# Low parts by VectorE, masks first, and other ranks for merged parts, in a fused attention and mixing kernel

## The chip, the core and the metric

The kernel runs on one core of one Trainium2 chip. The metric is the device time of one execution in microseconds (us); the figure quoted is the median of several runs. The engines are named as in the profile: PE is TensorE (PEld its weight loads), DVE is VectorE, ACT is ScalarE, POOL is GpSimd, SP is SyncE, which here only issues transfers.

## The reference

Three blocks follow each other, on batch 4, sequence 576, model width 512, all in fp32:

```python
# 1. attention in a window of 64, 8 heads of 64
scores = q @ k.T / 8;  keep 0 <= i - j < 64;  x = softmax(scores) @ v
# 2. four causal attention experts on x (width 64 each), the best two of four by a gate
q, k, v = x @ wq[e], x @ wk[e], x @ wv[e]
out += gate[e] * (softmax(causal(q @ k.T / 8)) @ v) @ wo[e]
# 3. mixing over tokens and channels
theta = x @ w_theta;  zr, zi = x * cos(theta), x * sin(theta)
u = x + w_tok_r @ zr + w_tok_i @ zi
return u + relu(u @ w_ch)
```

## The kernel before

**High and low parts.** Where fp32 accuracy is wanted, an operand is held as two tiles: a rounded high part, and a low part that is the difference. `split` (L101) makes them: one engine, mostly ScalarE, copies the high part (L103), another subtracts it from the source (L106). `mm3` (L108) then makes three matmuls of a product: high by high, high by low, low by high (L109 to L111). So each product needs both parts of both operands, and the low part is made after the high part.

**Stages.** Per batch b and, in the later stages, per half dh of the model width:
- `phase_a(b, hps)`: the windowed attention of block 1, in units of three blocks; scores to a bank (L297), mask and row minimum on VectorE (L305, which reads the masks ma0 and ma1 in the tile cst), exponential on ScalarE (L313), normalising on GpSimd (L320), transposes (L325, with the identity, also in cst), their copy pv (L328 on VectorE or L330 on ScalarE).
- `qk`, `vg_gates`, `attn(b, ep)`, `wo(b)`: projections, gates, the causal attention of two experts, and the output product of block 2. In `attn`, L493 scales by row on GpSimd or VectorE; the transposed diagonal block is copied on VectorE (L512) or ScalarE (L514).
- `fuse`: the product of wo and w_theta, in parts (tile wot). `load_tok`, `load_theta`, `load_ch`: weights, changed from float64 to parts.
- `theta(b, dh)`: angles (bank th), rounding on ScalarE and VectorE (L671, L672), sine and cosine on ScalarE (L674 to L676), product with the transposed x (bank xk) on VectorE (L679, or L693 for the last 64 tokens). For the first three halves the result is split into z (L683). For the other five, `sums_of` (L617) forms the operands of a Strassen product from two token tiles: X, W, Y and V, each with a high part on ScalarE; the low parts of X, W, Y are made at L627, L632 and L636, that of V at L644, and four sums and differences run on VectorE in between (L628, L629, L633, L637). It is called twice per half.
- `mix(b, dh)` for the first three halves and `mix7(b, dh)` for the other five: the product over tokens. Its banks are added to x2T by VectorE (L717, L785), and the sum u is split into cu (L718, L787). `halves` and `halves_end` make the differences of the token weights that `mix7` needs.
- `channel(b)`: the product over channels (bank c), read by VectorE (L843), then out.

**Order.** `merge` (L50) interleaves the parts of a stage: each part is a generator with a total; it yields costs, and the part whose (lead + cost so far) / total is smallest goes next. A larger total means that a part is taken earlier; a negative entry of LEAD puts a part in front, a positive one puts it back, as a share of its total. Parts are numbered in the order in which they are handed over, 0 to 67. This order gives ranks alone: at build time a planner simulates the engines and puts, on each engine, the ready instruction with the best rank next. On the chip each engine, and each engine's transfer queue, then runs its list in that fixed order. A PSUM bank is taken again only when its last reader is done (as 1, ta 1, g 2, bs 2, tb 2 banks).

**The start.** L251 to L254 issue the first transfers: on ScalarE's queue the first 256 columns of k (L251), then identity and masks together (L252); on SP's queue q and the rest of k. The next q and k tiles follow on SP's queue.

Of the kernel before, what the change touches and what calls it, by code (L numbers as in the profile page):

```python
# [23 lines left out]
DM = H * D  # L24
E = 4
NP = H // 2
KN = {'AT': [12.77, 1.06, 85.51, 5.4, 87.1, 55.86, 41.05, 4.07], 'QK': [15.5, 22.07, 12.32, 8.99, 4.97, 0.81, 9.98, 20.79, 20.6], 'VG': [18.37, 4.28, 3.79, 19.87], 'WO': [15.86, 4.2, 6.97, 88.79], 'PA': [11.6, 8.71, 12.47, 1.24, 2.53, 3.58, 5.67], 'TW': [0.76, 0.04, 2.9, 0.42, 2.07], 'CW': [14.78, 12.49, 0.86, 2.63, 1.4, 0.04, 1.33], 'SC': [5, 4, 5, 3, 0, 2, 1, 1], 'BD': [2, 1, 2, 1], 'PV': [0, 1, 2, 1], 'VB': [4, 0, 0, 2], 'WB': [0, 0, 0, 1], 'SB': 3, 'TB': 3, 'WOI': 0, 'AS': [0, 2, 1, 2], 'WE': [[0, 0], [0, 3], [0, 1]], 'XE': [0, 1, 1, 1], 'QB': [0, 1, 0, 0, 0, 0, 0, 0], 'DM': [1, 0, 0], 'DH': [1, 0, 0], 'DL': [0, 0, 1], 'BC': [1, 0, 1, 1], 'LT': 2, 'DP': [1, 1, 1], 'KC': 0, 'WM': 448, 'TC': [8.48, 13.11, 6.04, 7.5, 25.58, 9.0]}
TP = [8.14, 8.0]
CT = ("tb", "bs")
WARM = 2  # L30
LEAD = {19: 0.001, 22: -0.122, 29: 0.129, 35: -0.015, 36: -0.102, 38: 0.359, 42: 0.118, 43: 0.028, 51: -0.277, 54: 0.015, 67: -0.07}
MG = [20, 14.0, 4, 5, 12, 12, 13.0, 13.0, 13.0, 13.0, 13, 12]
TK0 = 1
THS = [[], [0], [], [1], [2], [3], [], []]
NB = S // 64
# [30 lines left out]
def kernel(ctx, tc, qT, kT, vw, consts, w_in, w_o, w_th, w_tk, w_ch, outT):  # L66
# [176 lines left out]
    def fetch(b, hp):  # L243
        if b == 0 and hp % 2:
            qt = bp.tile([P, D, NB], F32, tag="oh", bufs=3, name=f"qt{b}{hp}")
        else:
            qt = ap.tile([P, D, NB], F32, tag="qt", name=f"qt{b}{hp}")
        kt = ap.tile([P, S + 64], F32, tag="kt", bufs=2, name=f"kt{b}{hp}")
        if b == 0 and hp == 0:

            nc.scalar.dma_start(kt[:, :256], kT[b, hp, :, :256])  # L251
            nc.scalar.dma_start(cst[:, : 3 * P], consts[:, : 3 * P])  # L252
            nc.sync.dma_start(qt, qT[b, hp])
            last_load[0] = nc.sync.dma_start(kt[:, 256:], kT[b, hp, :, 256:])  # L254
        elif b == 0:
            nc.sync.dma_start(qt, qT[b, hp])
            last_load[0] = nc.sync.dma_start(kt, kT[b, hp])
        else:
            with tc.issue_after(last_v[0].ins):
                last_load[0] = nc.sync.dma_start(kt, kT[b, hp])  # L260
                nc.sync.dma_start(qt, qT[b, hp])
        return qt, kt
# [354 lines left out]
    def sums_of(b, dh, i, ang):  # L617
        A11, A21, A12, A22 = (ang[:, :, q, k] for q in range(2) for k in range(2))
        if i == 1:
            Z[b, dh] = {}  # L620
        ops = Z[b, dh]
        n = f"{b}{dh}{i}"
        st = (rp if i == 1 else kp).tile([P, 2, 2, P], F32, tag="z", name=f"s{n}")
        s1, s2 = st[:, :, 0], st[:, :, 1]
        x = operand(f"X{n}")
        nc.scalar.copy(out=x[1][:, 0], in_=ang[:, :, :, 0])
        p = nc.gpsimd.tensor_sub(out=x[1][:, 1], in0=ang[:, :, :, 0], in1=f32(x[1][:, 0]))  # L627
        nc.vector.tensor_add(out=s1, in0=A21, in1=A22)  # L628
        nc.vector.tensor_sub(out=s2, in0=s1, in1=A11)  # L629
        w = operand(f"W{n}")  # L630
        nc.scalar.copy(out=w[1][:, 0], in_=st)
        nc.gpsimd.tensor_sub(out=w[1][:, 1], in0=st, in1=f32(w[1][:, 0]))  # L632
        nc.vector.tensor_sub(out=A21, in0=A11, in1=A21)  # L633
        y = operand(f"Y{n}")
        nc.scalar.copy(out=y[1][:, 0], in_=ang[:, :, :, 1])
        nc.gpsimd.tensor_sub(out=y[1][:, 1], in0=ang[:, :, :, 1], in1=f32(y[1][:, 0]))  # L636
        nc.vector.tensor_sub(out=A12, in0=A12, in1=s2)  # L637
        if i == 1:
            tag = free.pop(0)
            ops["V"] = tag, slot(tag, [P, 2, 4, P], f"V{n}")  # L640
        v = ops["V"][1]
        sl = slice(i - 1, i + 1)
        nc.scalar.copy(out=v[:, 0, sl], in_=A12)
        nc.vector.tensor_sub(out=v[:, 1, sl], in0=A12, in1=f32(v[:, 0, sl]))  # L644
        for k, t in zip("XWY", (x, w, y)):
            ops[k, i // 2] = t
        return p

    def theta(b, dh):
        x2 = x2T[b]  # L650
        dsl = slice(dh * HW, dh * HW + HW)
        for i in range(4 if b % 2 else 5):
            n = f"{b}{dh}{i}"
            if i < 4:
                tok = slice(i * P, i * P + P)
                o = ring[8 * b + 4 * dh + i]
                load_o(1)
                x32, ow = (lambda c: x2[:, c, tok]), [o[:, k] for k in range(4)]
            else:
                xt, xo = XT[0]  # L660
                x32, ow = (lambda c: xt[:, c]), [xo[:, k] for k in range(4)]
            th = bank([P, HW], "bs", f"th{n}")
            for c in range(2):
                mm3(th, ow[2 * c], ow[2 * c + 1], GT[c][0][:, dsl], GT[c][1][:, dsl], c == 0, c == 1)
            xk = bank([P, HW], "tb", f"xk{n}")
            for c in range(2):
                nc.tensor.transpose(xk[:, c * P : (c + 1) * P], x32(2 * dh + c), ident)
            if i % 2 == 0:
                ang = bp.tile([P, 2, 2, HW], F32, tag="bms", bufs=2, name=f"ang{n}")
            rn, sn = ang[:, i % 2, 0], ang[:, i % 2, 1]  # L670
            nc.scalar.activation(out=rn, in_=th, func=AF.Identity, bias=magic)  # L671
            nc.vector.scalar_tensor_tensor(out=rn, in0=rn, scalar=-MAGIC, in1=th,  # L672
                                           op0=ALU.add, op1=ALU.subtract)
            nc.scalar.activation(out=sn, in_=rn, func=AF.Sin, scale=-TWO_PI)  # L674
            nc.scalar.activation(out=rn, in_=rn, func=AF.Abs)
            nc.scalar.activation(out=rn, in_=rn, func=AF.Sin, bias=halfpi, scale=-TWO_PI)  # L676
            if i < 4:
                both = ang[:, i % 2]
                d = nc.vector.tensor_mul(out=both, in0=xk.unsqueeze(1).to_broadcast([P, 2, HW]), in1=both)  # L679
                if 2 * b + dh < 3:  # L680
                    zt = slot(first[8 * b + 4 * dh + i], [P, 2, 2, HW], f"z{n}")
                    Z[b, dh, i] = zt
                    mark[b, dh, i] = d, split(zt[:, :, 0], zt[:, :, 1], both, nc.scalar, nc.gpsimd)  # L683
                elif i % 2:
                    mark[b, dh, i] = d, sums_of(b, dh, i, ang.rearrange("p j q (k n) -> p j q k n", k=2))
            else:
                for k in range(2):
                    zt = kp.tile([P, 1, 2, HW], F32R, tag=f"zt{k}{dh}", name=f"z{n}{k}")
                    Z[b + k, dh, i] = zt
                    z = (rp, kp)[k].tile([P, HW], F32, tag="z", name=f"zf{n}{k}")  # L690
                    r = slice(64 * k, 64 * k + 64)
                    for q, tr in enumerate((rn, sn)):
                        nc.vector.tensor_mul(out=z[64 * q : 64 * q + 64], in0=xk[r], in1=tr[r])  # L693
                    split(zt[:, 0, 0], zt[:, 0, 1], z, nc.scalar, nc.gpsimd)
            yield 1.5

    def mix(b, dh):
        x2 = x2T[b]
        if dh == 0:
            UH[b] = hl_set(utags, f"cu{b}")  # L700
        uh, ul = UH[b]
        y = [bank([P, 288], tag, f"y{b}{dh}{k}") for k, tag in enumerate(("g", "g", "as", "ta"))]
        for c in range(9):
            zt = Z[b, dh, c // 2]
            q = c % 2 if c < 8 else 0
            for k in range(4):
                n, mm = divmod(k, 2)
                sl = slice(288 * n, 288 * n + 288)
                ms = slice(mm * P, mm * P + P)
                mm3(y[k], zt[:, q, 0, ms], zt[:, q, 1, ms], wkh[c][:, sl], wkl[c][:, sl],  # L710
                    c == 0, c == 8)
            yield 1.45
        for k in range(4):
            n, mm = divmod(k, 2)
            m = 2 * dh + mm
            sl = slice(288 * n, 288 * n + 288)
            nc.vector.tensor_add(out=x2[:, m, sl], in0=y[k], in1=x2[:, m, sl])  # L717
            split(uh[m][:, sl], ul[m][:, sl], x2[:, m, sl], nc.scalar, nc.gpsimd)  # L718

    def halves():  # L720
        f1 = rp.tile([P, 4, 288], F32, tag="x2b", name="t1")
# [35 lines left out]
    def mix7(b, dh):  # L757
# [26 lines left out]
        def add(m, sl, g, ready=False):  # L784
            nc.vector.tensor_add(out=x2[:, m, sl], in0=g, in1=x2[:, m, sl])  # L785
            if ready:
                split(uh[m][:, sl], ul[m][:, sl], x2[:, m, sl], nc.scalar, nc.gpsimd)  # L787

        def spread(u, *homes):
            for m, sl in homes:  # L790
# [246 lines left out]
```

## Time and profile before

| | |
|---|---|
| median of 3 runs | 502.05 us (500.07 to 503.29) |
| the profiled execution | 501.43 us |
| its span, first to last instruction | 499.6 us |
| PE, PEld busy | 475.9, 446.2 us |
| DVE, ACT, POOL busy | 381.6, 342.2, 319.3 us |
| granted TensorE clock | 1.00 in every stretch |

The span is what the profile shows; the execution's time holds 1.8 us more around it. In the trace, phase_a for batch 0 fills the first 40 us or so, the stages of block 2 follow until about 285 us, and theta, mix, mix7 and channel take the rest. In a row of busy time, the number in brackets after it counts instructions. Matmuls overlap in the records, so a single matmul's time is longer than the step from one to the next.

### The profile page before, as it was taken

To read this page: it belongs to the slowest core of one execution; us is meant where nothing else is said; L and a number is where in the kernel's file an instruction comes from. 1 tells how busy PE (TensorE), PEld (TensorE's weight loads), DVE (VectorE), ACT (ScalarE), POOL (GpSimd) and SP (SyncE) were. 2 spreads that over 40 slices of the span, in tenths; PEclk is the share of its full clock that TensorE was granted. 3 is DMA by queue.
4 is the path that set the end of the run, shared out by engine and by line. 5 is a ranking of instruction groups with operands and counts; after the bars stand their busy time and mean duration, and the time that the engine had idled before them with its cause. 6 is when DMAs were issued, how large, how long until landed. Compare 5 with 4: busy or idle time off the path is not lost.

```text
span 499.6 us, 12071 instructions
## 1 busy us (share of the span) xinstructions
PE 475.9 (95%) x4128; PEld 446.2 (89%) x4128; DVE 381.6 (76%) x1283; ACT 342.2 (68%) x1054; POOL 319.3 (64%) x411
## 2 busy tenths in 40 slices
PE   7899899999999997999989999899999989999997
PEld 5689788999999897998878799899999989999997
DVE  6868989867779659877898969977668948893843
ACT  7948688867878756868787897876167717752620
POOL 6758789674776770323694556679558925891770
PEclk9999999999999999999999999999999999999999
DMA  8564253431316234112235953231362044202002
GB/s 272 182 227 134 67 179 108 139 100 49 125 60 198 78 97 147 33 38 92 88 120 168 349 176 144 71 78 43 100 175 65 23 143 131 65 22 96 2 0 96
DMA packets 45614, 55.92 MB, mean 112 GB/s; under 512 B 6641, under 2 KB 34289, under 8 KB 45553
## 3 DMA queue, kind: packets, MB, share of 16 engines
q1 hardware_dynamic: 44688, 52.46, 33.6%
q10 hardware_dynamic: 864, 2.69, 1.4%
q8 instruction: 33, 0.54, 0.4%
q14 instruction: 29, 0.23, 0.2%
HBM read 43.34 MB, written 11.80 MB: 110 GB/s over the span
## 4 chain that ended last, share of the span: by engine, by line
PE 52%; DVE 18%; ACT 15%; POOL 6%; issue 5%; DMA 3%; SPq 0%; DVEq 0%; ACTq 0%; POOLq 0%
PE as L297 3%; PE bpt L504 3%; ACT ams L313 2%; PE c L109 2%; PE c L110 2%; PE c L111 2%; PE apt L325 2%; PE qk L109 2%; PE bs L472 2%; PE qk L110 2%; PE ao L168 2%; PE qk L111 2%; PE bs L474 2%; PE o L522 2%; DMA wst<-in_dram 1%
## 5 line engine op out<-in xcount | busy, mean ns | idle before, releaser
L320 POOL TENSOR_TENSOR ams<-ams,arc 128x384 f32<-128x384 f32 x48 | 40.4, 845 | 34.4 <-DVE arc L319 14.3
L313 ACT ACTIVATE ams<-ams,anm 128x128 f32<-128x128 f32 x144 | 56.5, 396 | 4.0 <-DVE anm L305 2.9
L481 ACT ACTIVATE bms<-bms,bnm 64x64 f32<-64x64 f32 (+4 forms) x80 | 44.9, 562 | 13.1 <-DVE bnm L476 13.1
L297 PE MATMUL as<-kt,QD 128*128 128x128 f32 x288 | 41.2, 281 | 2.7 <-DVE anm L305 2.5
L297 PEld LDWEIGHTS as<-kt,QD 128*128 128x128 f32 x288 | 36.0, 192 | 6.2 <-DVE anm L305 2.9
L96 POOL TENSOR_SCALAR QD<-qt 64x576 f32<-64x576 f32 x24 | 30.6, 1274 | 11.7 <-DMA qt<-in_dram 4.6
L305 DVE CUSTOM_DVE_ANT_0 ams<-as,cst 128x128 f32<-128x128 f32 x144 | 34.1, 283 | 4.9 <-PE as L297 2.7
L476 DVE CUSTOM_DVE_ANT_0 bms<-bs,mb 64x64 f32<-64x64 f32 (+4 forms) x80 | 32.5, 422 | 5.4 <-PE bs L474 3.7
L106 POOL TENSOR_TENSOR cu<-x2T,cu 128x288 fp32r<-128x288 f32 x32 | 28.3, 901 | 9.9 <-ACT cu L103 9.8
L493 POOL TENSOR_SCALAR bpd<-bms,bsm,gw 128x64 f32<-128x64 f32 (+1 forms) x46 | 20.4, 445 | 20.2 <-DVE bsm L486 8.7
L109 PE MATMUL y<-wkh,z 128*128 128x288 f32 x108 | 32.1, 303 | 0.8 <-DVE x2T L717 0.8
L472 PE MATMUL bs<-KA,QS 128*128 128x288 f32 (+4 forms) x96 | 31.0, 331 | 1.1 <-DVE bnm L476 1.0
L110 PE MATMUL y<-wkl,z 128*128 128x288 f32 x108 | 31.9, 297 | 0.0
L679 DVE TENSOR_TENSOR ang<-xk,ang 128x512 f32<-128x512 f32 x32 | 21.6, 686 | 13.0 <-ACT ang L676 10.8
L111 PE MATMUL y<-wkh,z 128*128 128x288 f32 x108 | 30.9, 297 | 0.0
L671 ACT ACTIVATE ang<-th,magic 128x256 f32<-128x256 f32 x36 | 16.7, 470 | 18.8 <-PE th L111 17.7
L791 POOL TENSOR_TENSOR x2T<-x2T,u 128x288 f32<-128x288 f32 x20 | 16.9, 855 | 19.7 <-DVE u L802 18.1
L504 PE MATMUL bpt<-cst,bms 128*128 128x128 f32 x160 | 27.5, 276 | 1.5 <-ACT oh L103 1.5
L493 POOL TENSOR_SCALAR bms<-bms,bsm,gw 128x384 f32<-128x384 f32 (+3 forms) x38 | 24.7, 650 | 5.9 <-ACT wtuk L138 3.8
L474 PE MATMUL bs<-KL,QS 128*128 128x288 f32 (+4 forms) x96 | 28.4, 302 | 0.0
L313 ACT ACTIVATION_READ_ACCUMULATOR ams<-ams,anm 128x1 f32 x144 | 27.6, 192 | 0.0
L843 DVE SCALAR_TENSOR_TENSOR x2T<-c,x2T 128x288 f32<-128x288 f32 x32 | 13.8, 453 | 16.9 <-PE c L111 16.8
(337 smaller groups left out, 2051.7 us busy)
## 6 DMA issues: line engine op xcount, KB each, us to landing
vt<-in_dram SPq DMA_DIRECT2D x48, 192.0 KB, 2.9
or<-od SPq DMA_DIRECT2D x32, 256.0 KB, 3.3
kt<-in_dram SPq DMA_DIRECT2D x15, 320.0 KB, 3.1
qt<-in_dram SPq DMA_DIRECT2D x16, 288.0 KB, 3.6
out_dram<-x2T SPq DMA_DIRECT2D x32, 144.0 KB, 1.8
w64k<-in_dram SPq DMA_DIRECT2D x5, 576.0 KB, 4.2
od<-oh SPq DMA_DIRECT2D x8, 288.0 KB, 2.7
od<-ol SPq DMA_DIRECT2D x8, 288.0 KB, 2.8
```

Of the source, the lines that this page charges most:

```text
L109: nc.tensor.matmul(out, wh, xh, start=first, stop=False)
L110: nc.tensor.matmul(out, wh, xl, start=False, stop=False)
L111: nc.tensor.matmul(out, wl, xh, start=False, stop=last)
L297: nc.tensor.matmul(s[:, i, :], qd[:, blk], kt[:, 64 * blk : 64 * blk + 128], start=True, stop=True)
L305: nc.vector.tensor_tensor_reduce(out=ms[:, i, :], in0=s[:, i, :], in1=ma0 if (g == 0 and i == 0) else ma1, scale=-0.125, scalar=3.0e38, op ...
L313: nc.scalar.activation(out=ms[:, i, :], in_=ms[:, i, :], func=AF.Exp, bias=nm[:, i : i + 1], scale=-1.0, accum_out=sm[:, i, 0:1],)
L320: nc.gpsimd.tensor_mul(out=ms, in0=ms, in1=rc.unsqueeze(2).to_broadcast([P, 3, P]))
L472: nc.tensor.matmul(s[:, : z - a], qs[:, q0 : q0 + P], ka[:, a:z], start=True, stop=False)
L474: nc.tensor.matmul(s[:, : z - a], qs[:, q0 : q0 + P], KL[e][:, a:z], start=False, stop=True)
L481: ex = nc.scalar.activation(out=ms[:m, :w], in_=ms[:m, :w], func=AF.Exp, bias=nm[:m, ci : ci + 1], scale=-1.0, accum_out=ss[:m, i, 0:1])
L493: eng.tensor_scalar(out=dst, in0=src, scalar1=sm[:m, i : i + 1], scalar2=gw[:m, t, 2 * ep + i : 2 * ep + i + 1], op0=ALU.mult, op1=ALU.mult)
L504: nc.tensor.transpose(pt[:, jj, i, :], pn[:, i, P * j : P * j + P], ident)
```

## The change

1. The low parts of X, W and Y (L627, L632, L636), of z for the first three halves (L683) and of cu (L718, L787) are made on VectorE, not GpSimd. The low parts of the last 64 tokens' z and of the weights stay where they were.
2. The masks (128 KB) are the first transfer on ScalarE's queue, before k's first columns; the identity (64 KB) goes to SP's queue, behind the rest of k.
3. In tables, entry by entry:

| entry | before | after | what it sets |
|---|---|---|---|
| SC[3] | 3 | 5 | attn(1,1): all scalings of L493 on GpSimd, not only those of t >= 2 |
| BD[3] | 1 | 0 | batch 3: diagonal copies all on VectorE, not only those of odd t |
| PV[3] | 1 | 0 | phase_a(3): pv copies on VectorE, not ScalarE |
| AT[1], AT[2] | 1.06, 85.51 | 0.57, 63.46 | totals of attn(0,1), attn(1,0) |
| QK[0], QK[4], VG[3] | 15.5, 4.97, 19.87 | 15.22, 5.35, 50.45 | totals of qk(0,1), qk(2,1), vg_gates(3) |
| WO[0], WO[3] | 15.86, 88.79 | 17.82, 35.95 | totals of wo(0), wo(3) |
| PA[1], PA[2], PA[4] | 8.71, 12.47, 2.53 | 3.05, 9.33, 3.41 | totals of phase_a(2) in two stages, phase_a(3) |
| CW[4] | 1.4 | 1.72 | total of the first load_w |
| TC[0], TC[4] | 8.48, 25.58 | 9.88, 34.22 | totals of theta(0,1), and of mix in its stages |
| TP[1] | 8.0 | 6.68 | total of theta(3,0) and theta(3,1) |
| MG[5], MG[6] | 12, 13.0 | 27.74, 14.8 | totals of halves beside channel(0), theta(1,1) |

TC[3], MG[10] and MG[11] change too; the first isn't read, and the other two belong to parts that are merged with nothing. LEAD goes from 11 entries to 24. Its larger changes: part 24, attn(2,0), to -0.352; 37, load_tok beside attn(3,0), to -0.135; 38, attn(3,1), from 0.359 to none; 40, fuse, to 0.312; 45, theta(0,1), to 0.13; 48, theta(1,0), to 0.102; 54, theta(1,1), from 0.015 to -0.276; 61, mix7(2,1), to -0.373; 62, theta(3,0), to 0.438.

```diff
@@ fetch
+            nc.scalar.dma_start(cst[:, P : 3 * P], consts[:, P : 3 * P])
             nc.scalar.dma_start(kt[:, :256], kT[b, hp, :, :256])
-            nc.scalar.dma_start(cst[:, : 3 * P], consts[:, : 3 * P])
             nc.sync.dma_start(qt, qT[b, hp])
             last_load[0] = nc.sync.dma_start(kt[:, 256:], kT[b, hp, :, 256:])
+            nc.sync.dma_start(cst[:, :P], consts[:, :P])
@@ sums_of
-        p = nc.gpsimd.tensor_sub(out=x[1][:, 1], in0=ang[:, :, :, 0], in1=f32(x[1][:, 0]))
+        p = nc.vector.tensor_sub(out=x[1][:, 1], in0=ang[:, :, :, 0], in1=f32(x[1][:, 0]))
-        nc.gpsimd.tensor_sub(out=w[1][:, 1], in0=st, in1=f32(w[1][:, 0]))
+        nc.vector.tensor_sub(out=w[1][:, 1], in0=st, in1=f32(w[1][:, 0]))
-        nc.gpsimd.tensor_sub(out=y[1][:, 1], in0=ang[:, :, :, 1], in1=f32(y[1][:, 0]))
+        nc.vector.tensor_sub(out=y[1][:, 1], in0=ang[:, :, :, 1], in1=f32(y[1][:, 0]))
@@ theta
-                    mark[b, dh, i] = d, split(zt[:, :, 0], zt[:, :, 1], both, nc.scalar, nc.gpsimd)
+                    mark[b, dh, i] = d, split(zt[:, :, 0], zt[:, :, 1], both, nc.scalar, nc.vector)
@@ mix, and in the same way add() of mix7
-            split(uh[m][:, sl], ul[m][:, sl], x2[:, m, sl], nc.scalar, nc.gpsimd)
+            split(uh[m][:, sl], ul[m][:, sl], x2[:, m, sl], nc.scalar, nc.vector)
```

## Rows read from the trace of the kernel before

**Rows 1.** Stretches: start:end, length, then each engine's busy us (instructions), clock, transfers.

```profile
0.00:40.00 40.00, 34.31 (x328) 27.87 (x328) 28.57 (x141) 29.65 (x109) 26.51 (x52) 1.00 0.69 226
40.00:285.00 245.00, 235.60 (x2220) 216.34 (x2220) 198.58 (x857) 187.79 (x646) 154.00 (x232) 1.00 0.36 115
285.00:410.00 125.00, 119.69 (x919) 116.02 (x920) 95.94 (x180) 83.24 (x205) 86.21 (x78) 1.00 0.35 105
410.00:485.00 75.00, 75.00 (x580) 75.00 (x579) 54.09 (x98) 40.32 (x95) 50.08 (x48) 1.00 0.20 59
```

**Rows 2.** Waits of PE from 285 to 410: who, for whom, us, times, longest.

```profile
PE c L109 <- DVE zf L693: 1.3, 1, 1.3
PE th L109 <- DVE ang L672: 1.2, 1, 1.2
...
PE y L109 <- DVE x2T L717: 0.8, 2, 0.6
PE yh L109 <- DVE x2T L785: 0.7, 1, 0.7
```

**Rows 3.** Timeline at 398 to 401 us: start, duration, instruction, idle before it.

```profile
398.54 1.30 POOL L636 TENSOR_TENSOR Y<-ang,Y 128x512 fp32r<-128x512 f32 x1
398.58 1.53 DVE L644 TENSOR_TENSOR V<-ang,V 128x256 fp32r<-128x256 f32 x1
...
400.13 0.87 DVE L693 TENSOR_TENSOR zf<-xk,ang 64x256 f32<-64x256 f32 x2
...
401.14 0.37 PE L109 MATMUL c<-cu,wch 128*128 128x288 f32 x1 [1.26 <-DVE zf L693]
```

**Rows 4.** Timeline at 318 to 322 us, and at 385 us.

```profile
318.59 2.62 POOL L106 TENSOR_TENSOR z<-ang,z 128x512 fp32r<-128x512 f32 x2 [1.04 <-ACT z L103]
...
320.11 1.38 DVE L145 SCALAR_TENSOR_TENSOR wtuc<-w64c,wtuc 128x256 uint32<-128x256 uint32 x1
...
321.88 0.39 PE L109 MATMUL th<-wot,xo 128*128 128x256 f32 x1 [1.24 <-DVE ang L672]
...
385.49 1.30 POOL L627 TENSOR_TENSOR X<-ang,X 128x512 fp32r<-128x512 f32 x1 [0.32 <-ACT X L626]
385.70 1.37 DVE L629 TENSOR_TENSOR s<-s,ang 128x256 f32<-128x256 f32 x1
```

**Rows 5.** Two lines of one shape: ns shortest/median/longest, first and last start.

```profile
L629 DVE TENSOR_TENSOR s<-s,ang x10: 461/1132/1371, 369.6 to 473.1; 128x256 f32<-128x256 f32 x10
...
L672 DVE SCALAR_TENSOR_TENSOR ang<-ang,th x36: 403/409/422, 289.8 to 468.3; 128x256 f32<-128x256 f32 x36
```

**Rows 6.** Groups by line, 285 us on: count | busy us, mean ns | idle before, releasers.

```profile
L106 POOL TENSOR_TENSOR cu<-x2T,cu 128x288 fp32r<-128x288 f32 x32 | 28.3, 901 | 9.9 <-ACT cu L103 9.8
...
L627 POOL TENSOR_TENSOR X<-ang,X 128x512 fp32r<-128x512 f32 x10 | 13.7, 1369 | 4.6 <-ACT X L626 4.4 <-POOL cu L106 0.3
...
L629 DVE TENSOR_TENSOR s<-s,ang 128x256 f32<-128x256 f32 x10 | 10.7, 1072 | 0.0
...
L628 DVE TENSOR_TENSOR s<-ang 128x256 f32<-128x256 f32 x10 | 7.2, 724 | 0.1
...
L106 DVE TENSOR_TENSOR wot<-wot,wot 128x512 fp32r<-128x512 f32 x2 | 1.4, 680 | 0.0
...
L106 DVE TENSOR_TENSOR ttVD<-f,ttVD 128x288 fp32r<-128x288 f32 x2 | 0.9, 454 | 0.1
```

**Rows 7.** Groups by line: two copies on DVE, and GpSimd's scalings in the whole span.

```profile
L328 DVE COPY apv<-apt 128x384 f32<-128x384 f32 x16 | 8.8, 550 | 2.1 <-PE apt L325 2.0
...
L512 DVE COPY bpT<-bdt 128x128 f32<-128x128 f32 x8 | 2.2, 280 | 0.2 <-PE bdt L510 0.2
...
L493 POOL TENSOR_SCALAR bpd<-bms,bsm,gw 128x64 f32<-128x64 f32 (+1 forms) x46 | 20.4, 445 | 20.2 <-DVE bsm L486 8.7
```

**Rows 8.** Timeline of the first 8 us; ACTq and SPq issue transfers.

```profile
1.17 0.46 ACTq L252 DMA_DIRECT2D cst<-in_dram  x1
1.18 0.42 SPq L254 DMA_DIRECT2D kt<-in_dram  x1
...
5.93 1.24 ACT L292 COPY QD<-qt 64x576 f32<-64x576 f32 x1 [0.44 <-DMA qt<-in_dram]
...
7.20 0.40 ACT L313 ACTIVATE ams<-ams,anm 128x128 f32<-128x128 f32 x1
```

More of the change, by code (lines that the diff above doesn't have):

```diff
@@ L26 @@
 NP = H // 2
-KN = {'AT': [12.77, 1.06, 85.51, 5.4, 87.1, 55.86, 41.05, 4.07], 'QK': [15.5, 22.07, 12.32, 8.99, 4.97, 0.81, 9.98, 20.79, 20.6], 'VG': [18.37, 4.28, 3.79, 19.87], 'WO': [15.86, 4.2, 6.97, 88.79], 'PA': [11.6, 8.71, 12.47, 1.24, 2.53, 3.58, 5.67], 'TW': [0.76, 0.04, 2.9, 0.42, 2.07], 'CW': [14.78, 12.49, 0.86, 2.63, 1.4, 0.04, 1.33], 'SC': [5, 4, 5, 3, 0, 2, 1, 1], 'BD': [2, 1, 2, 1], 'PV': [0, 1, 2, 1], 'VB': [4, 0, 0, 2], 'WB': [0, 0, 0, 1], 'SB': 3, 'TB': 3, 'WOI': 0, 'AS': [0, 2, 1, 2], 'WE': [[0, 0], [0, 3], [0, 1]], 'XE': [0, 1, 1, 1], 'QB': [0, 1, 0, 0, 0, 0, 0, 0], 'DM': [1, 0, 0], 'DH': [1, 0, 0], 'DL': [0, 0, 1], 'BC': [1, 0, 1, 1], 'LT': 2, 'DP': [1, 1, 1], 'KC': 0, 'WM': 448, 'TC': [8.48, 13.11, 6.04, 7.5, 25.58, 9.0]}
-TP = [8.14, 8.0]
+KN = {'AT': [12.77, 0.57, 63.46, 5.4, 87.1, 55.86, 41.05, 4.07], 'QK': [15.22, 22.07, 12.32, 8.99, 5.35, 0.81, 9.98, 20.79, 20.6], 'VG': [18.37, 4.28, 3.79, 50.45], 'WO': [17.82, 4.2, 6.97, 35.95], 'PA': [11.6, 3.05, 9.33, 1.24, 3.41, 3.58, 5.67], 'TW': [0.76, 0.04, 2.9, 0.42, 2.07], 'CW': [14.78, 12.49, 0.86, 2.63, 1.72, 0.04, 1.33], 'SC': [5, 4, 5, 5, 0, 2, 1, 1], 'BD': [2, 1, 2, 0], 'PV': [0, 1, 2, 0], 'VB': [4, 0, 0, 2], 'WB': [0, 0, 0, 1], 'SB': 3, 'TB': 3, 'WOI': 0, 'AS': [0, 2, 1, 2], 'WE': [[0, 0], [0, 3], [0, 1]], 'XE': [0, 1, 1, 1], 'QB': [0, 1, 0, 0, 0, 0, 0, 0], 'DM': [1, 0, 0], 'DH': [1, 0, 0], 'DL': [0, 0, 1], 'BC': [1, 0, 1, 1], 'LT': 2, 'DP': [1, 1, 1], 'KC': 0, 'WM': 448, 'TC': [9.88, 13.11, 6.04, 6.76, 34.22, 9.0]}
+TP = [8.14, 6.68]
 CT = ("tb", "bs")
 WARM = 2
-LEAD = {19: 0.001, 22: -0.122, 29: 0.129, 35: -0.015, 36: -0.102, 38: 0.359, 42: 0.118, 43: 0.028, 51: -0.277, 54: 0.015, 67: -0.07}
-MG = [20, 14.0, 4, 5, 12, 12, 13.0, 13.0, 13.0, 13.0, 13, 12]
+LEAD = {8: -0.043, 19: -0.039, 22: -0.109, 24: -0.352, 29: 0.129, 30: -0.016, 31: -0.013, 35: -0.015, 36: -0.062, 37: -0.135, 40: 0.312, 42: 0.118, 43: 0.028, 45: 0.13, 47: 0.041, 48: 0.102, 51: -0.277, 53: -0.02, 54: -0.276, 58: 0.003, 61: -0.373, 62: 0.438, 63: 0.049, 67: -0.07}
+MG = [20, 14.0, 4, 5, 12, 27.74, 14.8, 13.0, 13.0, 13.0, 14.85, 6.56]
 TK0 = 1
@@ L786, in add @@
             if ready:
-                split(uh[m][:, sl], ul[m][:, sl], x2[:, m, sl], nc.scalar, nc.gpsimd)
+                split(uh[m][:, sl], ul[m][:, sl], x2[:, m, sl], nc.scalar, nc.vector)
         def spread(u, *homes):
```

## The prediction

> **What bounds the kernel now.** I read the stretches first. TensorE (PE) is busy 34.31 of the first 40 us, 235.60 of the next 245, 119.69 of 125 between 285 and 410, and all 75.00 of the 75 us up to 485 [rows 1]. So TensorE bounds nearly the whole kernel, and an edit can win only the time in which it stands idle: 5.7 us at the start, 9.4 us in the attention stages, 5.3 us in the first mixing stages, nothing from 410 to 485. The reader should see the sizes: the ceiling of any gain is about 20 us of 500, spread over many small gaps.
>
> The Trainium skill ("Trainium Kernel Development and Optimization", Performance Expectations) calls matmul busy time a bad measure of the distance to the limit and points to the share of weight loads. By that the room in 285 to 410 would be 125 - 116.02 = 9.0 us instead of 5.3. The rows from 410 on, where both stand at 75.00, show that the two agree where nothing stalls.
>
> Then the waits of TensorE between 285 and 410. Four groups, 4.0 us in all, end with a VectorE (DVE) instruction: th after L672, y after L717, yh after L785, c after L693 [rows 2]. None ends with GpSimd (POOL), so the low parts look harmless there. The timeline shows otherwise. At 398.58 VectorE starts L644, which takes 1.53 us, while GpSimd runs the low part L636 from 398.54 to 399.84. L693 stands behind L644 on VectorE's queue and frees the bank that the matmul at 401.14 waited 1.26 us for [rows 3]. The same picture stands at 320: GpSimd runs two low parts of z for 2.62 us, VectorE's L145 takes 1.38 us beside them, and TensorE then waits 1.24 us [rows 4]. The stall of yh has this form too: L629 takes 1.37 us at 385.70, beside the low part of X that began at 385.49 [rows 4]. So what GpSimd's low parts cost is paid on VectorE: L629, which reads two tiles in SBUF, ranges from 461 to 1371 ns, while L672, of the same 128x256 shape but with one operand in PSUM, stays within 403 to 422 ns [rows 5].
>
> **Low parts to VectorE.** 42 instructions of 128x512 (12 of z, 10 each of X, W, Y) and 32 of 128x288 (cu) leave GpSimd: 42 x 1.37 + 32 x 0.90 = 86 us of its 136 us between 285 and 485 [rows 1, 6]. VectorE takes them at 0.68 us (as wot does the same subtraction of 128x512) and 0.454 (ttVD, 128x288): 28.6 + 14.5 = 43.1 us [rows 6]. It gets back what it now loses beside them. The five instructions of a sum step (L628, L629, L633, L637, L644, ten times each) average between 724 (L628) and 1072 ns (L629) against about 415 undisturbed [rows 5, 6]: 0.31 to 0.66 us each, 15 to 33 us for the fifty, of which I take the middle, 24. VectorE's load from 285 to 485 goes from 150.0 us to 150.0 + 43.1 - 24 = 169 us of 200, or 85%: fuller, but not the bound. Per sum step it is even: three low parts add 2.04 us and five blocked instructions give back 5 x 0.48 = 2.4. Each half of a mixing product adds four cu low parts, 1.8 us on some 20 us.
>
> On the path of TensorE this removes the cause of the four stalls. I count 4.0 us for them, less 0.5 because VectorE now has a low part of its own in the queue: -3.5 us. The ends: -5.3 (all idle there goes) and, if low parts wait for their high part, the loss priced with the rivals.
>
> What GpSimd keeps (136 - 86 = 50 us in these 200) still reads SBUF. The Trainium skill ("SBUF — State Buffer", Who interferes with whom) says that a VectorE instruction with two SBUF inputs and a reading GpSimd instruction exclude each other, the later one waiting until the first is done; rows 3 and 5 agree, with L644 ending 0.27 us after L636. By that rule the refund is not whole: a quarter of the time is still taken by GpSimd, and 124 such instructions (74 new, 50 old) meeting it a quarter of the time for half of 0.9 us would wait 14 us, which puts VectorE at 92% and leaves less slack.
>
> The added wait: each low part now stands in VectorE's queue behind ScalarE's (ACT's) high part, and everything after it on VectorE (the evacuations L717, L785, L672 that free TensorE's banks) stands behind it. GpSimd waited 9.9 us for this on the 32 of cu and 4.6 on ten of X [rows 6], so VectorE could inherit from 0 to 9.9 + 42 x 0.46 = 29 us. I take a third, 10 us of waiting on an engine with 31 us to spare, since the planner sets other ready work in front.
>
> **Copies and scalings.** Twelve copies of pv for batch 3 and six diagonal copies go from ScalarE to VectorE: 12 x 0.550 and 6 x 0.280 = 8.3 us [rows 7] over 150 to 300 us, where work beside them on TensorE hides them; six scalings of attn(1,1), each at most 128 columns wide, go to GpSimd at about 0.45 us, 2.7 us in all [rows 7]. Cover gone, the copies would cost up to 1.5 us (a fifth of them exposed); a gain is bounded by the same figure, since ScalarE is relieved. I take 0.
>
> **The start.** The masks go first on ScalarE's queue, so k's first 256 columns are issued 0.46 us later; the identity is now third on SP's queue, in front of the second q tile, which moves by one issue of 0.42 us. That q tile matters: its copy on ScalarE, released by the transfer, runs from 5.93 to 7.17, and the first exponential starts at 7.20 [rows 8]. If the order stays, the start is 0.4 to 0.5 us late. If the planner puts the exponentials in front of that copy, because the masks are there, it gains up to 1.24 us. I take 0 and keep -1.2 to +0.5.
>
> **Leads and rates.** They add no work. They give parts of a stage another rank: attn(2,0) wholly first, theta(1,1) earlier, fuse later, mix7(2,1) earlier and theta(3,0) later, phase_a(2) later. What they can win is the idle of the stages they touch; 9.4 us before 285 bounds it below, and nothing excludes a loss of the same size. The nearest row is the stretch from 410, where merged parts of the same sort leave TensorE no idle time at all [rows 1]; so filling gaps is possible, and I take -2 us, a fifth of the idle.
>
> **Sum.** -3.5 + 0 + 0 - 2 = -5.5 us on the profiled execution of 501.4 us: 495.9. That execution lies 0.6 below the median of 502.05, so on the median 496.5.
>
> **Rivals.**
> - *Hidden anyway (no change).* The stalls removed are 4 us; new ones appear where VectorE is fuller, and the leads win nothing. For it: one stall of row 401.14's size in each of two or three stages gives back 2.5 to 3.8 us. Against it: the sum steps themselves get no longer. Time 498 to 505, centre 501.
> - *VectorE's queue stands behind ScalarE (slower).* Place: the five mix7 halves between 375 and 485, where TensorE has no slack. If the low parts inherit the whole 29 us, VectorE comes to 198 of 200 us and each half gets one stall like the 1.26 us one: 5 x 1.26 = 6.3 us, and none of the four old stalls is won net: 508. It decides once the wait per low part passes 24 / 74 = 0.32 us, where the refund is eaten. Cu's 9.9 / 32 = 0.31 on GpSimd speaks for it; that those waits were on an engine with time to spare speaks against.
> - *The masks do not help.* If VectorE's first masked reduction keeps its place behind the second q copy, that part of the change does nothing but delay: +0.5 us on the sum, 497.
>
> **How the numbers follow.** Faster as summed (490 to 497): 0.47. Hidden anyway, or a part of the sum only, between 497 and 507: 0.37. Slower by VectorE's queue, or by leads that lose: 0.16. The masks' rival, 0.4 by itself, shifts any of these by half a us to a us. One per cent, 5.0 us, is about what a measurement of this kernel can tell from no change. The likeliest case on its own spans 490 to 499. The range of 490 to 505 leaves out the slow case and a little at either end, two in ten.
>
> **What would show it.** Right: L629 and L644 near 0.42 us in most cases; GpSimd near 50 us between 285 and 485; no wait of TensorE over 1 us behind L672, L693 or L785; VectorE near 85% there. Wrong: VectorE idle before low parts with ScalarE's high part as the releaser, 20 us or more in total; TensorE stalls inside 410 to 485; a first exponential after 7.5 us; the attention stages before 285 longer than now, which would mean that the leads lose.

## The result, and the profile after

The changed kernel takes 494.8 us (median of 5 runs, 493.94 to 495.14), 0.986 of the kernel before (95% interval 0.983 to 0.988), which is 7.2 us less. The profiled execution took 494.8 us, its span is 492.9.

Stretches of the changed kernel, columns as in [rows 1] (start:end, length, then busy us and instructions of PE, PEld, DVE, ACT and POOL, clock, transfers):

```profile
0.00:40.00 40.00, 34.06 (x323) 27.54 (x323) 26.19 (x139) 28.38 (x103) 25.61 (x51) 1.00 0.71 223
40.00:285.00 245.00, 238.82 (x2249) 219.76 (x2250) 204.57 (x878) 186.35 (x639) 159.23 (x241) 1.00 0.38 119
285.00:410.00 125.00, 122.79 (x946) 119.05 (x945) 102.81 (x219) 82.74 (x204) 42.27 (x37) 1.00 0.34 101
410.00:485.00 75.00, 75.00 (x580) 75.00 (x579) 58.78 (x132) 39.46 (x93) 13.88 (x16) 1.00 0.20 59
```

Against [rows 1], TensorE does 27 more matmuls between 285 and 410 (946, not 919) and 24 more before 285 (2572, not 2548). From 285 to 485 GpSimd falls from 136 to 56 us, VectorE rises from 150 to 162.

Waits of TensorE from 285 to 410, all of them, against [rows 2]:

```profile
PE yi L109 <- DVE x2T L786: 0.8, 1, 0.8
PE bdt L511 <- DVE ol L106: 0.4, 1, 0.4
PE x L109 <- ACT xs3a L539: 0.3, 1, 0.3
PE xk L668 <- DVE ang L680: 0.2, 1, 0.2
```

The four waits of before are gone, and one of their kind is new (yi, 0.8 us). TensorE's idle time in the stretch falls from 5.3 to 2.2 us, of which these waits make 1.7. (From L255 on, line numbers are one higher than before.) The groups by line, as in [rows 6]:

```profile
L106 DVE TENSOR_TENSOR cu<-x2T,cu 128x288 fp32r<-128x288 f32 x32 | 14.6, 468 | 1.5 <-ACT cu L103 1.4
...
L106 DVE TENSOR_TENSOR z<-ang,z 128x512 fp32r<-128x512 f32 x12 | 11.1, 928 | 1.4 <-ACT z L103 1.4
...
L628 DVE TENSOR_TENSOR X<-ang,X 128x512 fp32r<-128x512 f32 x10 | 6.8, 680 | 0.0
...
L630 DVE TENSOR_TENSOR s<-s,ang 128x256 f32<-128x256 f32 x10 | 4.6, 464 | 0.0
L629 DVE TENSOR_TENSOR s<-ang 128x256 f32<-128x256 f32 x10 | 4.1, 414 | 0.0
```

L630 is the L629 of [rows 5]: 464 ns on the mean instead of 1072. The last column is the second thing to see: VectorE hardly waits for ScalarE's high parts, 1.5 and 1.4 us, where GpSimd had waited 9.9 for cu alone.

To say where the time came from, the times at which TensorE has done the same work are compared. The work of a matmul is the usual step to the next one of its form and bank in the trace before (the 25th percentile of these steps plus 5%, or their median if that is less). The table is worked out from the traces so. It gives us against the profiled execution before, minus is ahead; the heads are the times of before. A profile's start alone varies by some 0.8: e1 and e12 are as late at 103 as the changed kernel, with the old first transfers. Another value for a matmul's work moves the column 209 by up to 0.7, the others by 0.2 at most.

| kernel | 103 | 162 | 209 | 287 | 303 | 410 | 496 |
|---|---|---|---|---|---|---|---|
| changed | +0.8 | +0.9 | -3.1 | -3.4 | -1.8 | -6.2 | -6.5 |
| e1 low parts alone | +0.7 | +0.7 | +0.6 | +1.0 | +1.0 | -5.6 | -5.8 |
| e4 early ranks and switches | -0.4 | -0.3 | -4.3 | -3.2 | -2.4 | -2.5 | -2.5 |
| e7 changed, old late ranks | +0.5 | +0.6 | -3.4 | -3.7 | -2.0 | -7.9 | -8.0 |
| e8 low parts, early edits | -0.2 | -0.1 | -4.1 | -4.4 | -3.0 | -8.8 | -9.0 |
| e12 switches alone | +0.8 | +1.3 | -2.5 | -0.6 | +0.1 | -0.3 | -0.3 |

The changed kernel is 0.8 us late at the start, wins some 4 between 162 and 209, gives back 1.6 from 287 to 303, wins 4.4 from there to 410, and hardly anything moves after 410, where TensorE was full.

### The profile page after: what moved, and what is told of

Read it like the earlier page. It is cut to its first block, busy times and chain, and to the rows that moved or that the text cites. A ratio compares the mean times of both kernels' runs of the same rounds, so it can differ in the third digit from the quotient of the medians.

```text
span 492.9 us, 12028 instructions
## 1 busy us (share of the span) xinstructions
PE 475.5 (96%) x4128; PEld 445.9 (90%) x4128; DVE 394.2 (80%) x1369; ACT 336.9 (68%) x1036; POOL 241.0 (49%) x343
## 5 line engine op out<-in xcount | busy, mean ns | idle before, releaser
L792 POOL TENSOR_TENSOR x2T<-x2T,u 128x288 f32<-128x288 f32 x20 | 19.4, 982 | 80.5 <-ACT u L799 52.7
L494 POOL TENSOR_SCALAR bpd<-bms,bsm,gw 128x64 f32<-128x64 f32 (+1 forms) x50 | 22.4, 450 | 15.9 <-DVE ol L106 4.1
L672 ACT ACTIVATE ang<-th,magic 128x256 f32<-128x256 f32 x36 | 16.4, 470 | 15.9 <-PE th L111 11.7
L103 ACT CAST cu<-x2T 128x288 fp32r<-128x288 f32 x32 | 13.4, 430 | 18.1 <-DVE x2T L786 9.8
L326 PE MATMUL apt<-cst,ams 128*128 128x128 f32 x144 | 24.5, 277 | 1.3 <-ACT apv L331 0.6
```

The lines of the kernel that those rows point to most:

```text
L494: eng.tensor_scalar(out=dst, in0=src, scalar1=sm[:m, i : i + 1], scalar2=gw[:m, t, 2 * ep + i : 2 * ep + i + 1], op0=ALU.mult, op1=ALU.mult)
```

## The experiments

All times are medians, ratios are against runs of the kernel before on the same chip; differences between two experiments on different chips hold only as well as their ratios.

**e1 and e2: the low parts alone, and all but them.** e1 is the kernel before with part 1 of the change, e2 the changed kernel without it:

```diff
-        p = nc.gpsimd.tensor_sub(out=x[1][:, 1], ...   # and W, Y, z, cu
+        p = nc.vector.tensor_sub(out=x[1][:, 1], ...
```

> The kernel before with the low parts of X, W, Y, z and cu on VectorE, nothing else changed. Port theory (GpSimd's low parts hold up VectorE's two-input instructions, and those hold up TensorE): 3.0 to 4.4 us faster than before, about 498.4, all of it after 285 us; L629 and its like near 0.42 us. Rank theory (the leads and rates of the late stages win the time, the low parts only fit in): within 1 us of before, 501 to 503, since the planner's old ranks put the low parts where VectorE is needed.

> The changed kernel with the low parts put back on GpSimd. Port theory: 3.0 to 4.4 us slower than the changed one, about 498.5, and the sum steps' VectorE instructions back near 0.9 us on the mean. Rank theory: at most 1 us slower, about 495.5.

e1: 494.62 us, ratio 0.985 (0.981 to 0.989). e2: 499.39 us, 0.996 (0.994 to 0.998), 4.6 us above the changed kernel (5.0 by the ratios); its sum steps, the five VectorE instructions of `sums_of` beside the low parts, are back at 0.73 to 1.05 us on the mean. The rank theory falls: the low parts alone give 6.8 us, nearly as much as the whole change. The port theory (GpSimd's reading holds up VectorE's instructions with two operands in SBUF) has the sign and the place, but the size it gave was too small in e1. In e1, from 285 to 410:

```profile
285.00:410.00 125.00, 122.88 (x966) 121.28 (x966) 104.32 (x225) 84.74 (x212) 42.34 (x40) 1.00 0.36 111
```

966 matmuls instead of 919 [rows 1], in the same 125 us. Busy time of TensorE rises only by 3.2 us, that of its weight loads by 5.3: matmuls had been further apart before without a gap that the records show.

One thing e1 does not hold fixed. The planner lays the queues out anew for every kernel, and TensorE runs 724 of its 4128 matmuls at another place in its list than before, all from 304 us on (e2 against the changed kernel: 744). No run has the low parts on VectorE and the order of before, so what the new order gives of the 6.8 us is open. That the way back, e2, costs 4.6 speaks against mere luck.

**e5 and e6: what of it is the port.** On e1's kernel, GpSimd does each subtraction once more into a scratch tile (e5), or reads one column and then clears the scratch tile twice (e6):

```diff
+    def shadow(src, hi):      # called behind each low part, 256 or 288 columns
+        t = kp.tile([P, 288], F32, tag="shadow", name="shadow")[:, :n]
+        nc.gpsimd.tensor_sub(out=t, in0=src, in1=f32(hi))           # e5
+        nc.gpsimd.tensor_sub(out=t[:, :1], in0=src[one], in1=f32(hi[one]))  # e6
+        nc.gpsimd.memset(t, 0.0); nc.gpsimd.memset(t, 0.0)           # e6
```

> The kernel before with the low parts on VectorE, and GpSimd subtracts the same tiles once more into a scratch tile that nobody reads (116 subtractions, the same columns as before, about 86 us of GpSimd). Port theory: GpSimd's reading is what held VectorE up, so most of the 6.8 us gained by the low parts alone goes again, 498.5 to 502, and L629 and its like are near 0.9 us on the mean. Rival, latency theory (the gain is that a low part is ready 0.7 us earlier for TensorE): stays within 1 us of 494.6. The scratch results are extra work; the output is as before.

> As the kernel with the subtractions into scratch, but each of them reads one column only and is followed by two clearings of the scratch tile, so GpSimd is busy about as long and at the same places, and hardly reads. Port theory (it is the reading): within 1.5 us of 494.6, L629 near 0.45 us. If any GpSimd work beside VectorE costs, or GpSimd's queue itself (its adds for u stand behind): 498 to 501, as with the full subtractions.

e5: 523.56 us, 1.043 (1.038 to 1.048); e6: 510.57 us, 1.016 (1.012 to 1.021). Both missed: e5 is 29 us above e1, where 4 to 7 were expected. Groups by line from 285 us on, e5:

```profile
L106 DVE TENSOR_TENSOR z<-ang,z 128x512 fp32r<-128x512 f32 x12 | 13.4, 1127 | 0.6 <-ACT z L103 0.6
L647 DVE TENSOR_TENSOR Y<-ang,Y 128x512 fp32r<-128x512 f32 x10 | 11.3, 1131 | 0.0
...
L650 DVE TENSOR_TENSOR ang<-ang,s 128x256 f32<-128x256 f32 x10 | 8.2, 822 | 0.0
L644 DVE TENSOR_TENSOR ang<-ang 128x256 f32<-128x256 f32 x10 | 7.5, 751 | 0.0
```

and the same instructions in e6, with GpSimd's clearings:

```profile
L106 DVE TENSOR_TENSOR z<-ang,z 128x512 fp32r<-128x512 f32 x12 | 9.8, 820 | 0.8 <-ACT z L103 0.7
L648 DVE TENSOR_TENSOR Y<-ang,Y 128x512 fp32r<-128x512 f32 x10 | 7.0, 703 | 1.9 <-ACT Y L647 1.9
...
L645 DVE TENSOR_TENSOR ang<-ang 128x256 f32<-128x256 f32 x10 | 4.2, 418 | 0.0
L651 DVE TENSOR_TENSOR ang<-ang,s 128x256 f32<-128x256 f32 x10 | 4.2, 417 | 0.0
```

```profile
L623 POOL MEMSET shadow<- 128x288 f32 x232 | 78.8, 340 | 12.4
```

This shows that the reading holds VectorE up: beside 79 us of clearings the sum steps take 0.42 to 0.45 us, beside subtractions 0.59 to 0.82. GpSimd is about as busy in both (from 300 us on 152 us in e5, 156 in e6), so 13.0 us go with the reading at this load. By the reckoning of the table, between 303 and 410, where e1 wins 6.6 us, e6 still wins 3.4 and e5 loses 12.7. But e6 missed its expectation of 1.5 us by far, so the reading isn't all. Waits of VectorE from 285 us on in e6:

```profile
DVE u L820 <- POOL x2T L809: 7.8, 3, 3.0
...
DVE x2T L861 <- POOL shadow L621: 4.7, 8, 1.3
DVE x2T L802 <- POOL x2T L809: 3.9, 6, 1.0
```

GpSimd's adds of u into x2T (L791 before) stand behind whatever fills its queue, and VectorE waits for them. The second line comes from the shadows themselves, which hold x2T a little longer, so e6 overstates this path. And e6 loses its time elsewhere than e1 wins it: by the same reckoning 9.3 us go between 410 and 450, where e1 has no wait of TensorE at all. Waits of TensorE from 285 us on in e6, the two longest, both mostly in these 40 us:

```profile
PE th L109 <- DMA or<-od: 2.1, 1, 2.1
PE th L109 <- DVE ang L686: 2.0, 2, 1.7
```

One of them is for a transfer. The planner's order differs here too (853 matmuls against e1, 805 between e5 and e6), so not all of e6's 16 us, nor all of the 13.0, need be GpSimd's. How the 6.8 us divide between reading, queue and order is not settled by the two. The traces of before and e1 show some of the queue's share: from 285 to 485 VectorE's waits for GpSimd fall from 11.5 to 6.2 us, the adds taking 1.4 of that and L736, which waits for GpSimd's L733, 4.2; its sum steps get 23.5 us shorter.

**e9 to e11: the three kinds of low part, each alone,** on the kernel before:

```diff
+        nc.vector.tensor_sub(...)      # e9: X, W, Y (30)
+  split(zt[:, :, 0], zt[:, :, 1], both, nc.scalar, nc.vector)    # e10: z (12)
+  split(uh[m][:, sl], ul[m][:, sl], x2[:, m, sl], nc.scalar, nc.vector)   # e11: cu (32)
```

> The kernel before with the 30 low parts of X, W and Y alone on VectorE. Port theory by stage: in the run with all low parts the stretch of the sum steps, from 369 us on, won 3.6 us, so 2.5 to 3.6 us faster than before, about 499. If the gain was GpSimd's queue in front of its adds for u and not the port: the same place, so the sign doesn't tell these two apart, but the adds (L791) would then show VectorE waiting less for them. If the three kinds only win together: within 1 us of before.

> The kernel before with the 12 low parts of z alone on VectorE. Port theory: the stalls behind L145 at 320 us and behind L736 at 341 us go, 1.5 to 3 us faster than before, about 500, all between 300 and 360 us. If z's part on VectorE stands in the way as much as it frees: within 1 us of before.

> The kernel before with the 32 low parts of cu alone on VectorE. The prediction counted these as a load of 0.45 us each that gives nothing back: 0 to 1 us slower or the same, 502. If they hold VectorE up as the others do (they stand beside the sum steps too): 1 to 2 us faster, 500.5.

e9: 501.54 us, ratio 1.000 (0.997 to 1.002). e10: 499.92, 0.997 (0.994 to 0.999). e11: 506.03, 1.007 (1.004 to 1.010). Singly they sum to -0.5 - 2.1 + 4.0 = +1.4 us against 502.03; together they gave -6.8. z alone wins, X, W and Y alone do nothing, cu alone loses, which its expectation had at 1 us at most. e10 hits its place: 2.7 us are won between 303 and 369 us. e9 leaves a stall like that of [rows 3] where it was, from another cause: L693 there stands behind the low parts of W and Y on VectorE, 0.69 and 0.68 us. Waits of TensorE from 285 on in e9, and then in e11:

```profile
PE c L109 <- DVE zf L693: 1.5, 1, 1.5
PE th L109 <- DVE ang L672: 1.2, 1, 1.2
```

```profile
PE th L109 <- DVE ang L672: 1.2, 1, 1.2
PE c L110 <- DVE cu L106: 1.2, 1, 1.2
PE c L109 <- DVE ang L679: 1.2, 1, 1.2
PE yh L109 <- DVE x2T L785: 0.9, 1, 0.9
```

The stalls behind L672 and L785 are those of before. e11 loses its 3 us between 415 and 455, where TensorE was full before; the wait behind L679 stands there. In e11 the low parts themselves are held up, and of the sum steps L633 as before:

```profile
L106 DVE TENSOR_TENSOR cu<-x2T,cu 128x288 fp32r<-128x288 f32 x32 | 19.5, 621 | 1.3 <-ACT cu L103 1.2
L633 DVE TENSOR_TENSOR ang<-ang 128x256 f32<-128x256 f32 x10 | 9.9, 993 | 0.0
```

In e9, with cu and z still on GpSimd, the sum steps get most of their time back:

```profile
L629 DVE TENSOR_TENSOR s<-s,ang 128x256 f32<-128x256 f32 x10 | 6.1, 611 | 0.0
...
L633 DVE TENSOR_TENSOR ang<-ang 128x256 f32<-128x256 f32 x10 | 5.4, 537 | 0.0
```

Of the 44.9 us of the five sum-step lines e9 takes off 16.6, e11 5.3 and e10 nothing: 21.1 in sum, against 23.5 in e1. So the refund nearly adds up. The load does not: low parts that move alone are held up by the kinds that stay, and cost 24.4 (e9), 9.7 (e10) and 19.5 us (e11), 53.6 in sum, against 47.1 in e1. That these 9 us of VectorE make the 8.2 us between +1.4 and -6.8 is not shown; the planner's order differs between all of these kernels as well. VectorE's busy time does not order the kernels either: from 285 to 485 it is 159.4 us in e11, the slowest of these, and 163.5 in e1, the fastest.

**e4 and e12: the stages before the mixing.** e4 is the kernel before with the entries of KN for these stages, LEAD up to 40 and the three switches; e12 has the switches alone:

```diff
-'SC': [5, 4, 5, 3, ...], 'BD': [2, 1, 2, 1], 'PV': [0, 1, 2, 1]
+'SC': [5, 4, 5, 5, ...], 'BD': [2, 1, 2, 0], 'PV': [0, 1, 2, 0]
```

> The kernel before with the changed ranks and the three switches (SC, BD, PV) of the stages before the mixing alone. Theory that these stages won about 4 us between 162 and 209 us and gave 1 to 1.5 us back by 303: 2 to 3.5 us faster than before, about 499.3. Rival (that gain came from the shifted start or from what the later stages let in ahead): within 1 us of before.

> The kernel before with SC[3], BD[3] and PV[3] as changed and no other edit. If the copies of pv taken from ScalarE in phase_a(3) won the time at 160 to 210 us: 2 to 2.5 us faster than before, as with all early edits. If the ranks won it: within 1 us of before, or up to 1.5 us slower from the copies on VectorE.

e4: 499.0 us, 0.994 (0.992 to 0.996), as expected. e12: 500.97, 0.998 (0.995 to 1.000). The stretch 150 to 215 us, before and then e12:

```profile
150.00:215.00 65.00, 61.20 (x596) 56.94 (x591) 50.41 (x230) 46.81 (x169) 32.68 (x48) 1.00 0.34 107
```

```profile
150.00:215.00 65.00, 64.48 (x640) 60.19 (x637) 54.99 (x253) 46.94 (x175) 35.28 (x56) 1.00 0.35 113
```

The switches alone fill this stretch, 3.8 us by the table between 162 and 209, and lose most of it again by 303; with the new ranks (e4), 2.1 us are left there from 162 on. So the switches, costed at nothing, open the gain, and the ranks seem to keep part of it: e4 is 1.4 us ahead of e12, but their intervals overlap. Which of the three switches it is was not tested.

**e3, e7 and e8: the start and the late ranks.** e3 is e1 with the new first transfers. e7 is the changed kernel with TC, TP, MG, WO[3] and LEAD from 41 on as before; e8 is e7 with the old first transfers:

```diff
-TP = [8.14, 6.68]
+TP = [8.14, 8.0]      # e7; and so on for MG, TC, WO[3], LEAD 41 and up
```

> The kernel before with the low parts on VectorE and the new order of the first transfers. Theory that the start loses (the identity in front of the second q tile on SP's queue): 0.5 to 1.2 us slower than with the low parts alone, all of it in the first 40 us. Rival (the planner uses the early masks once other things don't stand in the way): the same or up to 1 us faster than with the low parts alone.

> The changed kernel with the ranks from theta(0,0) on as before (TC, TP, MG, WO[3] and the entries of LEAD from 41 on). Theory that the late ranks give back what the low parts and the early stages won (6.8 + 2.4 - 0.6 for the start = 8.6 in sum, against 7.2 measured): 1 to 2 us faster than the changed kernel, about 493.3. Rival (the gains do not add, since both fill the same idle time): within 0.7 us of 494.8; if the late ranks help: 496 to 497.

> The kernel before with the low parts on VectorE and the ranks and switches of the stages before the mixing. If the gains add: 502 - 6.8 - 2.4 = 492.5 to 493. If they fill the same idle time: 494 to 495. Against the one that has the new order of the first transfers as well: 0.3 to 0.8 us faster if that order costs.

e3: 495.25 us, 0.989 (0.984 to 0.993). e7: 493.27, 0.982 (0.978 to 0.986). e8: 493.0, 0.982 (0.978 to 0.986). With the new first transfers the kernels are 0.6 us (e3 against e1) and 0.3 us (e7 against e8) slower, and TensorE's order is the same in each pair; the intervals overlap, so this is a tendency only. e8 lands where its sum puts it, at 492.5 to 493: low parts -6.8 and early edits -2.4 add up. The late ranks' +1.5 is the difference of the changed kernel and e7, 494.8 - 493.3, and stands between 303 and 410 by the table. It seems to hold only beside the low parts: e2, with these ranks and without the low parts, is 2.0 us faster than the kernel before, where -2.4 + 1.5 + 0.3 would leave 0.6. e8 was the fastest of all kernels here, 1.8 us below the changed one, though the intervals of e7 and e8 just overlap with its.

## Why the prediction came out as it did

The sign was right and the forecast of 496.5 us came within 1.7 us of the 494.8 measured, the sum less so: its terms were -3.5 (low parts), 0 (start), 0 (switches) and -2 (ranks); measured apart they are -6.8, +0.3 to +0.6, and -2.4 + 1.5 = -0.9 for ranks and switches. The low parts were forecast 3.3 us too small and the rest some 1.5 us too large. That the two errors offset each other in part is luck. The term that was mis-sized most is that of the low parts.

- **Low parts, -3.5 forecast, -6.8 measured.** The mechanism was right as far as it is shown: the four stalls went, L629 fell from 1072 to 464 ns, and e5 beside e6 shows that GpSimd's reading makes these instructions long. That this alone makes the 6.8 us is not shown; queue and order stand beside it. The size was wrong because the bound of -5.3 us was taken from idle time. The sentence on the Trainium skill ("Trainium Kernel Development and Optimization", Performance Expectations) gave 9.0 us from the weight loads' share, and I let the idle time decide because the two agree from 410 on. e1 shows the stretch from 285 to 410 doing 47 more matmuls with 3.2 us more busy time: here the Trainium skill's measure held, and the measured 6.8 lies between 5.3 and 9.0.
- **Refund of 24 us on VectorE.** The five lines took 44.9 us before and 22.3 us after: 22.6 us. Load added: 43.1 forecast, 47.3 measured, as z's low parts took 0.93 us each, not 0.68; eight of the twelve took 0.68 or 0.69, but four, beside what GpSimd still reads for the weights, 0.93 to 1.91 us. VectorE came to 161.6 of 200 us, 81% instead of 85%: lines outside the sum steps got time back too (L139 went from 5.5 to 3.0 us), and some work may have moved ahead of 285, where the kernel was 3.4 us early.
- **What GpSimd keeps.** Forecast 50 us, measured 56. The rule of the Trainium skill ("SBUF — State Buffer", Who interferes with whom) is borne out further by e6: a GpSimd instruction that only writes does not hold VectorE's two-input instructions up (0.42 to 0.45 us in the sum steps beside 232 clearings). The one instruction of [rows 3] fits a hold over the whole instruction less well: L644 ends 0.27 us after L636 and takes some 0.41 alone; spans on GpSimd are rough.
- **The added wait behind ScalarE.** I took 10 us of a bound of 29; 2.9 us were measured. The rival of a slower kernel rested on it and falls. That a kind of low part alone could be 4.0 us slower (e11) was in no rival: I counted every low part at its undisturbed time, but one that moves alone is held up by the kinds that stay, cu by 0.62 against 0.47 us.
- **The start.** Bounds -1.2 to +0.5. The exponentials did not move in front: the first starts at 7.31 us, 0.11 later than in [rows 8], and at 7.53 and 7.63 in e3 and e7, against 7.11 to 7.48 in the kernels with the old first transfers. The second q tile can come later still: in e2's profile, the slowest of its ten runs, its copy on VectorE starts at 8.01, not 5.93. One tile on there is another delay. The copy of the third q tile in the kernel before and in the changed one:

```profile
10.04 0.73 DVE L294 COPY QD<-qt 64x576 f32<-64x576 f32 x1
```

```profile
11.60 0.71 DVE L295 COPY QD<-qt 64x576 f32<-64x576 f32 x1 [1.40 <-DMA qt<-in_dram]
```

  In e7 it starts at 11.55, in e8, which has the old first transfers and is otherwise the same, at 10.45; in e3 at 10.34, in e1 at 10.13. So the new transfers delay this copy by 1.1 us beside the early ranks and by 0.2 without them, and the times of these pairs differ by less than their intervals.
- **Leads and rates, -2 forecast.** The early part won, together with the switches; the late part lost 1.5 us beside the low parts. The row I called the nearest, 410 to 485, could not show this: TensorE was full there either way.

## What to carry to other kernels

Where one engine's reading holds up another, look for the cost on the other engine, by comparing instructions of one shape with one and with two operands in SBUF. Do not judge such a move by its parts: three partial moves here gave -2.1 to +4.0 us, all together -6.8. When a planner orders the queues, every edit is also another order, and a run that keeps the order is needed to tell the two apart; for the low parts none here does. Take the ceiling of a gain from counts of matmuls per stretch or from the weight loads, not from TensorE's idle time. Ranks that suit a kernel before an edit are worth trying again after it: here the old late ranks were 1.5 us better than the new, with intervals that just overlap.

## What had not been expected of the hardware

A kernel with GpSimd load that reads next to nothing was still much slower: e6, with 79 us of clearings and 33 of one-column subtractions, is 16 us above e1, which has the same VectorE work; how much of this is the planner's other order is open. A one-column subtraction took 0.25 to 0.33 us there. And VectorE can be busier and the kernel faster: 163.5 us in e1 against 150.0 before, in the same 200 us.
